# Both feed-forward layers by seven half-size products per 576-token batch, with weight operands streamed from DRAM

## The chip, the cores and the metric

One NeuronCore of a Trainium2 chip runs the whole program. The engines are named as in the profile: PE (TensorE), DVE (VectorE), ACT (ScalarE), POOL (GpSimd) and SP (SyncE, which here only issues DMAs). The metric is the device time of one execution in microseconds; lower is better. Everything is computed in fp32.

## The reference

Attention over 8 batches of 8 heads, 576 tokens, head size 64, with a threshold on the scores, then a feed-forward block over all 8 x 576 = 4608 tokens. The two feed-forward weights arrive as 64-bit floats.

```python
scores = q @ k.T / 8                                   # per batch and head, 576 x 576
scores = where(scores >= max(scores) - tau, scores, -1e9)
attn = exp(scores - max(scores)); attn /= sum(attn) + 1e-9
x = (attn @ v) as (4608, 512)                          # heads side by side
h = x @ w_in                                           # (4608, 512) @ (512, 2048)
out = (h / (1 + exp(-1.702 * h))) @ w_out              # (4608, 2048) @ (2048, 512)
```

## The kernel before, in words

**Attention.** The work goes by *pairs* of heads: 32 pairs, four to a batch. Of a pair `n`, `load_qk` and `load_v` fetch the data, `prep` (L522) transposes q and k in 32 x 32 blocks, `scores` (L538) makes the transposed scores in nine steps `j`, each four matmuls of 288 columns on the four 64 x 64 quarters of PE's array, and `keep` (L555) copies each step out of PSUM on ACT. Scores lie in tiles of two steps (1152 columns), the ninth step alone. `in_groups` (L561) takes maxima over keys on DVE, `sub` (L666) subtracts the row's threshold, `mask` (L672) and `exps` (L676) on ACT finish it, `in_groups` again sums, `values` (L687) multiplies by v on PE, and `place_x` (L789) divides and writes the result, already transposed, into `xT`. For pairs 0 to 4 the sums are made on PE (`sums_by_pe`). From pair 7 on (`JOINT`) the values of pair n - 2 and the scores of pair n run on PE in turn as one uninterrupted stretch.

**Feed-forward.** Tokens go in 18 blocks of 256, which don't match the batches of 576 (`cuts`). Three forms are used:

- Blocks 0 and 1, plain: `mm1_0` (L844, 256 columns), `tanh` on ACT, `gelu_0` on DVE (x times sigmoid as 0.5 x (1 + tanh)), `mm2` (L826, 512 columns).
- Blocks 2 to 13 (`feed_forward`): layer one plain in `mm1` (L804), layer two by seven products of half size (Strassen's scheme in Winograd's form) in `product` (L995). Its operand sums of the activations are made on POOL (`s_sums` L961 to L963, `s_last` L974), those of `w_out` once (`t_minus`, `t_plus`). DVE adds the products together as it reads them from PSUM (`read`, L1017).
- Blocks 14 to 17 in two pairs (`two_blocks`): both layers by seven products, layer one in `product1` (L909, read by `read1`, L925), layer two in `product`. The sums of `w_in` for this are made in SBUF that attention has left.

In a seven-product scheme a matrix product is cut into 2 x 2 quarters, and 7 products of quarters replace 8, at the price of sums of operands and of results.

**Weights.** Both weight matrices stay in SBUF from the start. Each of 32 pieces is loaded twice by POOL (L473, L474, 512 KB each, the second shifted by three bytes) and turned from 64-bit to 32-bit by three steps on DVE and one on ACT (`cv_ex` L484, `cv_power` L492, `cv_frac` L498 and L502, `cv_end` L510). Six staging places are in use.

**PSUM.** Two pools: `psA`, three tiles of two banks (scores, values, some products), and `psM`, two tiles of one bank (feed-forward, early sums).

**What sets the order.** Every step is a task with an engine, an assumed cost, a rank, predecessors and places that it takes and gives back. `run_in_order` simulates these tasks and lets each free engine take the ready task of lowest rank; the instructions are emitted in that order, so each engine's queue is fixed when the kernel is built. Attention tasks have rank `n` plus an offset by function name (`EARLY` for pairs 0 to 3, `SECOND` for 4 to 7, `LATER`, and `CV` for the conversions; ranks below zero get none). Matmuls of the feed-forward have rank 1000 (`LAST`), so on PE attention goes first whenever it is ready. `LEAD` = 6 holds attention back: the scores of pair n wait for feed-forward task 16 (n - 6), so attention runs some six pairs ahead and ends well before the feed-forward does.

Of the kernel before, what the change touches and what calls it, by code (L numbers as in the profile page):

```python
# [19 lines left out]
P = 128  # L20
# [10 lines left out]
def kernel(  # L31
# [13 lines left out]

# [3 lines left out]
    NPAIR = H // 2  # L69
    KT = P // 2  # L70
    NK = S // KT
    NKT = NK // 2
    SH = S // 2
    QB = S // 32
    BLK = 256
    BANK = 512
    HT = BLK // 2
    HF = d_ff // P // 2
    HM = d_model // 2
    NBLK = B * S // BLK  # L80
    NDC = d_model // P
    NFC = d_ff // P
    SCALE = 1.0 / math.sqrt(D)

# [4 lines left out]
    work = ctx.enter_context(tc.tile_pool(name="work", bufs=2))  # L89
# [3 lines left out]
    psA = ctx.enter_context(tc.tile_pool(name="psA", bufs=3, space=bass.MemoryType.PSUM))  # L93
    psM = ctx.enter_context(tc.tile_pool(name="psM", bufs=2, space=bass.MemoryType.PSUM))

    w_in = const.tile([P, NDC, d_ff], FP32, name="w_in")
    w_out = const.tile([P, NFC, d_model], FP32, name="w_out")

    N_T, N_G, N_S = 3 * HF * HM, NFC * BLK, 2 * HF * HT
    arena = const.tile([P, N_T + N_G + N_S], FP32, name="arena")
    tw = [arena[:, ts(x, HF * HM)].rearrange("p (j m) -> p j m", m=HM) for x in range(3)]
    g = arena[:, ds(N_T, N_G)].rearrange("p (f j t) -> p f j t", f=2, t=BLK)
    sg = [
        arena[:, ds(N_T + N_G + x * HF * HT, HF * HT)].rearrange("p (j t) -> p j t", t=HT)
        for x in range(2)
    ]
# [8 lines left out]
    minus = const.tile([P, 2, KT], FP32, name="minus")  # L117
    own_row = const.tile([P, QB // 2], FP32, name="own_row")
    shift = const.tile([P, 1], FP32, name="shift")

    tasks = []
    NXT = 5
    limits = {"psA": 3, "psM": 2, "s_m": 8, "s_t": 2, "io": 2, "hs": 2, "osb": 2, "xT": NXT, "mb": 1,
              "raw0": 1, "raw1": 1, "qkT0": 1, "qkT1": 1, "v_m0": 1, "v_m1": 1, "w64_0": 1, "w64_1": 1, "row": 1, "row_s": 1, "rc": 1}
    for x in ("raw0", "raw1", "qkT0", "qkT1", "mb"):
        limits[x + "_apart"] = 1  # L130
    limits["s_m_apart"] = NKT

    EARLY = {
        "exps": -17.61,
        "in_groups": 12.77,
        "keep": 26.48,
        "load_qk": 6.42,
        "load_v": 0.46,  # L140
        "mask": 4.73,
        "one_group": -15.86,
        "one_row": -9.06,
        "over_halves": -11.42,
        "over_tiles": -0.06,
        "place_x": -9.61,
        "prep": -11.56,
        "row_in": 31.26,
        "row_out": -12.68,
        "scores_run": 26.41,  # L150
        "spread_max": 4.27,
        "spread_sums": 4.87,
        "sub": 8.56,
        "sums_by_pe": -5.69,
        "sums_in": 2.27,
        "sums_out": 16.51,
        "turn_rows": -16.86,
        "turn_sums": -5.4,
        "values": 24.67,
        "w_sum": 2.1,  # L160
        "x_sum": -20.63,
    }
    SECOND = {
        "exps": -12.92,
        "in_groups": 29.73,
        "keep": 6.19,
        "load_qk": 1.9,
        "load_v": 13.07,
        "mask": 1.29,
        "one_group": 2.55,  # L170
        "one_row": -2.79,
        "over_halves": -24.79,
        "over_tiles": 9.26,
        "place_x": -19.31,
        "prep": -22.42,
        "row_in": -9.56,
        "row_out": -26.33,
        "scores_run": 2.45,
        "spread_max": 6.39,
        "spread_sums": -1.67,  # L180
        "sub": 27.62,
        "sums_by_pe": 38.88,
        "sums_in": 16.9,
        "sums_out": 8.98,
        "turn_rows": 12.04,
        "turn_sums": -0.33,
        "values": 2.02,
        "w_sum": -3.88,
        "x_sum": -12.22,
    }  # L190
    LATER = {
        "exps": 1.49,
        "in_groups": 1.97,
        "keep": -9.78,
        "load_qk": -5.98,
        "load_v": -3.59,
        "mask": 21.95,
        "one_group": 4.78,
        "one_row": -20.84,
        "over_halves": 8.94,  # L200
        "over_tiles": -3.1,
        "place_x": 4.68,
        "prep": -7.1,
        "row_in": 2.23,
        "row_out": -2.52,
        "scores_run": -13.43,
        "spread_max": -3.68,
        "spread_sums": -27.9,
        "sub": 9.4,
        "sums_by_pe": 4.28,  # L210
        "sums_in": 8.55,
        "sums_out": -0.12,
        "turn_rows": -4.72,
        "turn_sums": 8.12,
        "values": 0.63,
        "w_sum": 21.55,
        "x_sum": 7.65,
    }
    CV = {
        "cv_end": -26.29,  # L220
        "cv_ex": 6.34,
        "cv_frac": -13.49,
        "cv_power": -9.91,
        "load_w": 3.03,
# [4 lines left out]
    QUARTERS = ("scores", "scores_run", "again", "values", "sums_by_pe")  # L229
    ENTER = {True: 0.2, False: 0.22}  # L230

    def task(engine, cost, rank, f, *a, after=(), take=(), give=(), lag=None):
        if lag is None:
            lag = LAG[engine]
        if 0 <= rank < LAST:
            biases = EARLY if a[0] < NPAIR else SECOND if a[0] < 2 * NPAIR else LATER
            rank += CV[f.__name__] if f.__name__ in CV else biases.get(f.__name__, 0.0)
        tasks.append((engine, cost, rank, f, a, [x for x in after if x is not None],
                      take, give, lag))
        return len(tasks) - 1  # L240
# [103 lines left out]
    rebias = const.tile([P, 1], FP32, name="rebias")  # L344
    JOINT = 7
    TWICE = ()
    BY_POOL = {}

    APART = (1, 3)
    spare = arena[:, 8 * P * 4 :]
    offset = {"raw0": 0, "raw1": S, "qkT0": 2 * S, "qkT1": 3 * S, "mb": 4 * S}
    offset.update({f"s_m{t}": (6 + 2 * t) * S for t in range(NKT)})

    room, end = {}, 0
    for tag, size, bufs in (
        ("s_m", 2 * S, 8), ("s_t", S, 2), ("raw0", S, 1), ("raw1", S, 1), ("qkT0", S, 1),  # L360
        ("qkT1", S, 1), ("mb", S, 1), ("rc", S, 1), ("v_m", NK * 2 * D, 2),
    ):
        room[tag] = [(end + x * size, size) for x in range(bufs)]
        end += bufs * size
    arena2 = const.tile([P, end], FP32, name="arena2")
    held = {}

    def seat(tag, x=0):
        o, size = room[tag][x]
        return arena2[:, o : o + size]  # L370

    def home(n, tag, key=None):
        if n in APART:
            o = offset[key or tag]
            return spare[:, o : o + (2 if tag == "s_m" else 1) * S]
        return seat(tag)

    def seat_scores(n, t):

        if t < NKT and n in APART:  # L380
            return home(n, "s_m", f"s_m{t}")
        if n >= JOINT:
            tag, o, size = held[n, t] = held.pop((n - 2, t))
            return arena2[:, o : o + size]
        tag = "s_m" if t < NKT else "s_t"
        o, size = room[tag].pop(0)
        held[n, t] = tag, o, size
        return arena2[:, o : o + size]

    def free_scores(n, tiles=range(NKT + 1)):  # L390
# [5 lines left out]
    def own(n, *pools):  # L396
        return tuple(x + "_apart" for x in pools) if n in APART else pools


# [28 lines left out]
    WC = 512  # L428
    wide = moe_w_in.dtype != FP32
    pieces = [(w_in, moe_w_in, c, j) for j in range(d_ff // WC) for c in range(NDC)]  # L430
    n_in = len(pieces)
    pieces += [(w_out, moe_w_out, c, j) for c in range(NFC) for j in range(d_model // WC)]
# [1059 lines left out]
```

## Time and profile before

| | |
|---|---|
| runs | 1311.93, 1314.18, 1315.43 us; median 1314.18 |
| profiled execution, span from first to last instruction | 1309.8 us |
| median of the runs less that span | 4.4 us |
| mean granted clock of PE | 0.989 |
| DMA | 103.78 MB in 194309 packets, 160284 of them under 512 B |
| first feed-forward matmul (L844) | 113.9 us |
| first matmul of a block with seven products (L804) | 273.6 us |
| last write into `xT` (L789) | 1081.0 us |
| end of the last matmul | 1306.2 us |

The profiled execution lists a span and no time of its own; the runs' times hold 4.4 us beside it, by their median. In a group's line the profile gives the source line, engine, operation, operands with shapes, the count, then busy us and mean ns of one instruction, then the engine's idle time before them and what ended it. An fp32 matmul has two records, so counts of matmuls are half the records. DMA-issuing instructions don't count as busy.

### The profile page before, as it was taken

To read this page: it belongs to the slowest core of one execution; us is meant where nothing else is said; L and a number is where in the kernel's file an instruction comes from. 1 tells how busy PE (TensorE), PEld (TensorE's weight loads), DVE (VectorE), ACT (ScalarE), POOL (GpSimd) and SP (SyncE) were. 2 spreads that over 40 slices of the span, in tenths; PEclk is the share of its full clock that TensorE was granted. 3 is DMA by queue.
4 is the path that set the end of the run, shared out by engine and by line. 5 is a ranking of instruction groups with operands and counts; after the bars stand their busy time and mean duration, and the time that the engine had idled before them with its cause. 6 is when DMAs were issued, how large, how long until landed. Compare 5 with 4: busy or idle time off the path is not lost. (4 is left out here: it accounts for less than half of the span.)

```text
span 1309.8 us, 22824 instructions
## 1 busy us (share of the span) xinstructions
PE 1260.5 (96%) x9128; PEld 972.6 (74%) x9128; DVE 1002.2 (77%) x1601; ACT 646.6 (49%) x830; POOL 246.1 (19%) x300
## 2 busy tenths in 40 slices
PE   5869999999999999999999999999999999999998
PEld 2436854477688777777778888777777778888887
DVE  7999998989998877778877877777888864652642
ACT  5975656766664544455554545454556540210210
POOL 1301210022030212112020302020212117120120
PEclk8989999999999999999999999999999999999999
DMA  6976967264322222221222222222122110000000
GB/s 118 339 186 214 282 209 132 67 125 83 82 57 71 55 64 64 56 57 44 63 47 61 55 71 55 72 56 70 42 52 54 38 44 9 9 1 33 1 1 32
DMA packets 194309, 103.78 MB, mean 79 GB/s; under 512 B 160284, under 2 KB 171292, under 8 KB 194204
## 3 DMA queue, kind: packets, MB, share of 16 engines
q1 hardware_dynamic: 180476, 64.30, 20.6%
q0 software_dynamic: 11360, 37.74, 9.7%
q8 instruction: 71, 1.16, 0.4%
q10 hardware_dynamic: 2368, 0.30, 0.2%
q14 instruction: 34, 0.28, 0.1%
HBM read 88.40 MB, written 9.70 MB: 75 GB/s over the span
## 5 line engine op out<-in xcount | busy, mean ns | idle before, releaser
L561 DVE TRANSPOSE_TENSOR_REDUCE part<-arena 128x36 f32<-128x1152 f32 x295 | 361.5, 1241 | 45.9 <-ACT arena L555 32.3
L804 PE MATMUL hps<-xT,w_in 128*128 128x256 f32 x1536 | 336.9, 380 | 0.4 <-DVE arena L816 0.4
L804 PEld LDWEIGHTS hps<-xT,w_in 128*128 128x128 f32 x1536 | 290.8, 190 | 45.5 <-issue 5.7
L672 ACT ACTIVATE arena<-arena 128x1152 f32<-128x1152 f32 (+1 forms) x160 | 169.4, 1058 | 144.9 <-DVE arena L666 144.6
L555 ACT COPY arena<-ps 128x576 f32<-128x576 f32 x288 | 170.4, 647 | 121.2 <-PE ps L538 120.9
L666 DVE TENSOR_TENSOR arena<-arena 128x1152 f32<-128x1152 f32 (+1 forms) x158 | 197.5, 1281 | 19.6 <-DMA arena<-row 19.5
L995 PE MATMUL ops<-w_out,arena 128*128 128x256 f32 x896 | 202.9, 381 | 1.2 <-DVE arena L816 1.1
L676 ACT ACTIVATE arena<-arena,shift,scl 128x1152 f32<-128x1152 f32 (+1 forms) x160 | 200.1, 1251 | 4.1
L538 PE MATMUL ps<-arena 64*64 64x288 f32 x2304 | 174.1, 419 | 25.1 <-DVE arena L522 14.4
L995 PEld LDWEIGHTS ops<-w_out,arena 128*128 128x128 f32 x896 | 169.0, 190 | 29.1 <-DVE arena L816 3.7
L961 POOL TENSOR_TENSOR arena<-arena 128x256 f32<-128x256 f32 x56 | 50.8, 907 | 658.4 <-DVE arena L816 556.7
L687 PE MATMUL pv<-arena 64*64 64x288 f32 x2176 | 161.2, 410 | 0.0
L538 PEld LDWEIGHTS ps<-arena 64*64 64x64 f32 x2304 | 83.7, 137 | 93.6 <-ACT arena L555 30.7
L995 PE MATMUL ops<-arena 128*128 128x256 f32 x672 | 150.6, 380 | 0.0
L813 ACT ACTIVATE th<-hps 128x512 f32<-128x512 f32 x112 | 66.0, 589 | 167.9 <-PE hps L804 148.2
L995 PEld LDWEIGHTS ops<-arena 128*128 128x128 f32 x672 | 127.3, 190 | 19.3 <-issue 2.2
L687 PEld LDWEIGHTS pv<-arena 64*64 64x64 f32 x2176 | 82.0, 135 | 55.3 <-issue 12.8
L1017 DVE SCALAR_TENSOR_TENSOR osb<-ops,osb 128x256 f32<-128x256 f32 x98 | 39.5, 414 | 91.8 <-PE ops L995 85.0
L816 DVE SCALAR_TENSOR_TENSOR arena<-th,hps 128x512 f32<-128x512 f32 x96 | 64.1, 667 | 37.1 <-ACT th L813 37.0
L844 PE MATMUL hps<-xT,w_in 128*128 128x256 f32 x256 | 57.3, 382 | 1.3 <-DVE arena L850 1.2
L826 PE MATMUL ops<-w_out,arena 128*128 128x512 f32 x128 | 56.4, 596 | 0.0
L844 PEld LDWEIGHTS hps<-xT,w_in 128*128 128x128 f32 x256 | 48.1, 190 | 11.0 <-DVE arena L850 3.0
(117 smaller groups left out, 1027.8 us busy)
## 6 DMA issues: line engine op xcount, KB each, us to landing
arena<-in_v_dram SPq DMA_DIRECT2D x128, 144.0 KB
arena<-in_q_dram SPq DMA_DIRECT2D x128, 72.0 KB
out_dram<-osb SPq DMA_DIRECT2D x36, 256.0 KB
arena<-in_k_dram SPq DMA_DIRECT2D x124, 72.0 KB
arena<-row SPq DMA_DIRECT2D x62, 144.0 KB
arena<-row_s SPq DMA_DIRECT2D x54, 144.0 KB
w_out<-in_moe_w_in_dram POOLq DMA_DIRECT2D x12, 512.0 KB, 9.4
arena<-in_moe_w_out_dram POOLq DMA_DIRECT2D x12, 512.0 KB, 5.9
```

The source lines that it names most:

```text
L538: nc.tensor.matmul(ps[ts(c, KT), h, 0:SH], lhsT=mats[n, 1][ts(h, D), ts(j, KT)], rhs=mats[n, 0][ts(h, D), ts(c, SH)], start=True, stop=True,)
L555: nc.scalar.copy(out=sT[n, t][:, u], in_=pss.pop((n, j))[:, :, 0:SH])
L561: nc.vector.tensor_reduce(out=stats[n, op][:, t * 2 * QB : min(2 * t + 2, NK) * QB], in_=sT[n, t].rearrange("p u h (g d) -> p (u h g) d", ...
L666: engine.tensor_tensor(out=s, in0=s, in1=mbs[n].unsqueeze(1).to_broadcast(list(s.shape)), op=ALU.subtract)
L672: nc.scalar.activation(out=s, in_=s, func=AF.Prelu, alpha=STEEP)
L676: nc.scalar.activation(out=s, in_=s, func=AF.Exp, scale=scl, bias=shift)
L687: nc.tensor.matmul(o[c][ts(h, D), 0:SH], lhsT=left(j, h)[ts(c, KT)], rhs=sT[n, t][ts(c, KT), u, h, :], start=(j == 0), stop=(j == NK - 1),)
L804: nc.tensor.matmul(hidden[j][:, ts(f, BLK)], lhsT=w_in[:, c, ds((f * HF + j) * P, P)], rhs=xTs[blk][:, c, :], start=(c == 0), stop=(c == N ...
L813: nc.scalar.activation(out=ths[j], in_=hidden[j], func=AF.Tanh, scale=GELU_SCALE / 2)
L816: nc.vector.scalar_tensor_tensor(out=g[:, :, j, :], in0=two(ths.pop(j)), scalar=1.0, in1=two(hidden.pop(j)), op0=ALU.add, op1=ALU.mult,)
L844: nc.tensor.matmul(hidden[j][:, ts(i, BLK)], lhsT=w_in[:, c, ts(j, P)], rhs=xTs[i][:, c, :], start=(c == 0), stop=(c == NDC - 1),)
L995: nc.tensor.matmul(banks[blk][k][:, ts(o, HM)], lhsT=left[:, j, :], rhs=right[:, j, :], start=(j == 0), stop=(j == HF - 1),)
```

## The change

- Feed-forward goes by batches of 576 tokens instead of blocks of 256. All matmuls of it have 288 columns (half a batch).
- The first batch is plain (`product0`, `product00`, 16 x 8 matmuls each). The other seven go by seven products in both layers: `product1` for four pairs of row blocks `jp`, `product2` for two column halves `i`. Results come out transposed, are turned on DVE (`turn_out`) and stored in runs of 32 numbers.
- Weights: the 32 pieces are quarters, four to a *quad*; eight quads. They are converted into `weights`, the first batch uses them there; POOL makes the four sums of each quad (`w_sum`), and the seven operands of each quad go to DRAM (`store_base`, `store_sums`). Every later batch loads them again in *cells* of two 512-column operands, seven cells in a ring (`load_cell`, issued by POOL). The SBUF of `weights` then holds `g`.
- Sums of x (`x_sum`) and of g (`g_sum`, four per `jp`), and the gelu of two of four quarters, go on POOL; for the latter ACT adds the one (`plus_one`). DVE does the other two and all reads from PSUM.
- One PSUM pool of four slots with two banks serves everything. `values` of a pair, scores and products all take a slot.
- Attention's tiles are three of three steps (1728 columns) instead of four of two and one of one; `place_x` is one instruction.
- Loads of weights use three staging places instead of six. Pairs 4 and 5 load q and k into free space of `xT`.
- All offsets of ranks are replaced, and `LEAD` becomes 5.38, counted in feed-forward time (27.16 us per pair); the sums of `w_out` in SBUF, the `two_blocks` form and unused variants go.

The core of the diff:

```diff
-    psA = ctx.enter_context(tc.tile_pool(name="psA", bufs=3, space=bass.MemoryType.PSUM))
-    psM = ctx.enter_context(tc.tile_pool(name="psM", bufs=2, space=bass.MemoryType.PSUM))
+    psum = ctx.enter_context(tc.tile_pool(name="psum", bufs=1, space=bass.MemoryType.PSUM))
+    TILES = (3, 3, 3)
+    NCELL = 7
+    NHS = 5
+    slots = [0, 2, 4, 6]
...
+    def load_cell(key):
+        _, kind, x, k = key
+        c = at[key] = cells.pop(0)
+        if kind == 0:
+            rows = w_dram[x].rearrange("p (a w) -> p a w", w=U)
+            rows = (rows[:, 0:4:3], rows[:, 1:5:3], rows[:, 5:7], rows[:, 2:3])[k]
+            o = cell(c).rearrange("p (a w) -> p a w", w=U)
+            CELL_ON.dma_start(out=o[:, 0 : rows.shape[1]], in_=rows)
...
+    P1, P6, P2, P7, P5, P3, P4 = range(NQ)
+    def product1(b, jp, x):
+        b11, b12, b21, b22 = (x_quarter(b, d, t) for d in range(2) for t in range(2))
+        right = {P1: b11, P6: xsum[1], P2: b21, P7: b12, P5: xsum[0], P3: b22, P4: xsum[2]}[x]
+        c = cell(at[b, 0, jp, x // 2])[:, ts(x % 2, U)].rearrange("p (c j f) -> p c j f", c=2, j=2)
+        bank = banks[x] = slot()
+        for u in range(2):
+            for d in range(2):
+                nc.tensor.matmul(
+                    ps_all[:, bank + u, 0:SH], lhsT=c[:, d, u, :], rhs=right[:, d, :],
+                    start=(d == 0), stop=(d == 1),
+                )
...
+    SUMS = {P6: (1, 0), P2: (0, 0), P7: (2, 1), P3: (1, 1), P4: (2, 2)}
+    def read1(x, part=0):
+        ps = scored(banks[x])[:, :, 0:SH]
+        if x == P1:
+            hs[0] = hs_free.pop(0)
+            nc.scalar.copy(out=hs[0], in_=ps)
...
+        o, i = SUMS[x] if x != P5 else ((1, 1), (3, 2))[part]
+        nc.vector.tensor_tensor(out=hs[o], in0=ps, in1=hs[i], op=ALU.add)
...
+    G_SUMS = ((4, 1, 0), (5, 3, 4), (1, 3, 1), (6, 2, 5))
+    def g_sum(jp, k, engine):
+        o, a, c = (g[:, jp, y] for y in G_SUMS[k])
+        engine.tensor_tensor(out=o, in0=a, in1=c, op=ALU.subtract)
...
+    def product2(b, i, x, h):
+        right = {P1: 0, P6: 5, P2: 2, P7: 1, P5: 4, P3: 3, P4: 6}[x]
+        c = cell(at[b, 1, i, x])[:, ts(h, U)].rearrange("p (j m) -> p j m", m=P)
+        for j in range(4):
+            nc.tensor.matmul(
+                ps_all[:, banks[x], 0:SH], lhsT=c[:, j, :], rhs=g[:, 2 * h + j // 2, right, j % 2, :],
+                start=(j == 0 and h == 0), stop=(j == 3 and h == 1),
+            )
...
+    def store(b, i, m, o):
+        for y in range(4):
+            nc.sync.dma_start(
+                out=out[ds(b * S, S), ds((2 * m + i) * P + 32 * y, 32)].rearrange(
+                    "(t a) m -> a t m", a=32
+                ),
+                in_=ot[o][ts(y, 32)].rearrange("p (t m) -> p t m", m=32),
+            )
...
-    LEAD = 6
+    LEAD = 5.38
+    W_RANK = (-11.09, -0.32, 24.62, -9.57, -4.22, 9.2, 81.56, -23.12)
+    CELL_ON = nc.gpsimd
+    X_ON, G_ON, T_ON, W_ON = "POOL", ("POOL", "DVE", "POOL", "DVE"), "POOL", "POOL"
...
+        for jp in range(NJP):
+            loads = [load((b, 0, jp, y), [jp], 2.0 if y < 3 else 1.0) for y in range(4)]
...
+            for y in range(4):
+                after = [gs[jp, z] for z in range(4)] + ([tsum[jp, y - 1]] if y else [])
+                tsum[jp, y] = task(
+                    T_ON, 1.45 if T_ON == "POOL" else 0.67, FIRST, g_sum, jp, y, engines[T_ON], after=after,
+                )
...
+                for h in range(2):
+                    after = ffn[-1:] + [a]
+                    for jp in (2 * h, 2 * h + 1):
+                        if x in (P1, P2, P3):
+                            after.append(gs[jp, {P1: 0, P2: 2, P3: 3}[x]])
+                        else:
+                            after.append(tsum[jp, {P6: 1, P5: 0, P7: 2, P4: 3}[x]])
...
+    PER_PAIR = 32 * NQ * FF / NPAIR
```

## The prediction

> **What bounds the kernel now.** I read four views in this order: the busy times of the whole execution, the chain that ended last, the waits of TensorE, and the busy times cut into stages. The cuts are the first feed-forward matmul (113.9 us), the first one of a seven-product block (273.6), the last attention write into `xT` (1081.0) and the end of the last matmul (1306.2).
>
> ```profile
> PE 1260.5 (96%) x9128; PEld 972.6 (74%) x9128; DVE 1002.2 (77%) x1601; ACT 646.6 (49%) x830; POOL 246.1 (19%) x300
> ```
>
> TensorE (PE) is busy 96% of 1309.8 us. Busy matmuls overlap in the records, so I check this against spacing. In the chain that ended last the columns are start, length, line, count:
>
> ```profile
> 1257.80 24.17 PE ops L995 x112
> 1281.98 24.19 PE ps L995 x112
> ```
>
> A matmul has two records, so 56 matmuls of 256 columns take 24.17 us: 0.4316 us each. In the middle, attention runs values and scores in turn:
>
> ```profile
> 604.06 1.15 PE L538 MATMUL ps<-arena 64*64 64x288 f32 x16
> 605.03 1.15 PE L687 MATMUL pv<-arena 64*64 64x288 f32 x16
> 606.00 1.15 PE L538 MATMUL ps<-arena 64*64 64x288 f32 x16
> ```
>
> Sixteen records are two sets of four quarter-array matmuls, and the next set starts 0.97 later: a pass of 288 columns takes 0.485, which is also 0.4316 x 288/256. So both column counts have a price.
>
> ```profile
> 0.00:113.90 113.90, 76.22 (x1008) 40.71 (x1008) 102.16 (x178) 85.34 (x108) 20.89 (x52) 0.90 0.78 215
> 113.90:273.60 159.70, 155.66 (x1037) 96.45 (x1034) 145.81 (x237) 93.56 (x119) 21.04 (x34) 0.99 0.63 173
> 273.60:1081.00 807.40, 803.57 (x6049) 638.14 (x6048) 650.35 (x989) 439.33 (x547) 149.52 (x162) 1.00 0.26 60
> 1081.00:1306.20 225.20, 225.09 (x1042) 197.31 (x1040) 103.49 (x202) 28.35 (x56) 54.63 (x52) 1.00 0.03 11
> ```
>
> After length come PE, weight load, VectorE (DVE), ScalarE (ACT), GpSimd (POOL), clock, DMA share, GB/s. PE idles 37.7 us before the first feed-forward matmul, where DVE is 90% busy, and only 8 us in all behind it. From 273.6 on I can rebuild the time: 1888 feed-forward matmuls (in units of 256 columns) x 0.4316 = 815, 22 pairs of scores and 24 of values x 9 x 0.485 = 201, sum 1016 of 1032.6; the rest is mode changes and 4 us of idle. **PE is the bound from 114 us to the end**; attention's other engines fit beside it.
>
> **The change, part by part.** The sum goes against the profiled 1309.8, which lies 4.4 below the median of 1314.18; I add that back.
>
> *Matmuls.* Before: 2 plain blocks 256 (128 in `mm1_0`, 64 of double width in `mm2`), 12 blocks x (64 `mm1` + 56 `product`) = 1440, 2 double blocks x (112 `product1` + 112 `product`) = 448; 2144 x 0.4316 = 925.3 us. After: first batch 16 x 8 + 16 x 8 = 256 of 288 columns, seven batches x (4 x 7 x 4 + 2 x 7 x 8) = 224 each, 1824 x 0.485 = 884.6. Attention keeps its passes (32 x 18, sums of 5 pairs). **-40.7 us**, all on the path. Weight loads (190 ns each) stayed under the spacing of 216 ns and have 242.
>
> *Start.* Before 113.9 DVE converts 16 pieces of `moe_w_in` at 0.42 + 0.43 + 0.70 + 0.69 = 2.24 us, 36 us in all. After, the loads go in one chain through three staging buffers, and quad 2 stands at rank 24.6 behind early attention; only quad 0's four pieces (with quads 0 and 1, eight) must be done by the first product. Seven or eight conversions moved behind that point free up to 16 us of DVE, but the next stage has DVE at 91% and must take them. Against it: 14.7 MB of operands are written to DRAM, and pieces are read in rows of 1 and 2 KB instead of 4. The first two stages used 0.78 x 113.9 + 0.63 x 159.7 = 189 us of all 16 DMA engines out of 273.6; 14.7 MB at the rate of queue 0 below is 49 more, the accumulating copies that go give back 13. 225 still fits. Bounds -12 and +15; I take -3, nearer to no change, since what moves lands in a nearly full stage.
>
> *VectorE and PSUM.* By the forms of the groups:
>
> ```profile
> L925 DVE TENSOR_TENSOR arena<-ps,arena 128x256 f32<-128x256 f32 x68 | 27.5, 421 | 15.9 <-PE ps L909 15.0
> L961 POOL TENSOR_TENSOR arena<-arena 128x256 f32<-128x256 f32 x56 | 50.8, 907 | 658.4 <-DVE arena L816 556.7
> L974 POOL TENSOR_TENSOR arena<-arena 128x512 f32<-128x512 f32 x28 | 35.6, 1271 | 102.3 <-PE ops L995 102.3
> ```
>
> Pieces of `place_x` (L789) grow 1.06 ns per column, so a read of 576 columns is 0.76 us. Per batch: 28 such reads 21.3, 8 gelus x 0.75 = 6.0, 14 reads of 288 x 0.45 = 6.3, 4 transposes x 0.745 = 3.0: 36.6, against 2.25 x (8 x 0.676 + 7 x 0.424) = 18.9 before. Tiles of three give back 5 (an L561 of 1728 columns is 1.97; 24 fewer starts). So +13 us per batch, and DVE goes from 81% to some 91% while attention runs. Between 360 and 393 us the present kernel has DVE at 97% with PE at 100% (31.7 and 32.7 of 32.7 us), so this can be hidden; I charge **+3**, bounds 0 and +15. All four PSUM slots of two banks now serve both users, and a product needs 1.94 us where its read needs 0.76 (P5: 1.5), so reads keep up on average.
>
> *GpSimd and the handover.* 28 operations of 576 columns (727 ns at 256 and 1271 at 512 in undisturbed calls give 1.41) are 39 us a batch, and 30 issues of cells at 0.54 to 0.65 are 18: 40% of some 145 us, but 80% of layer one's 54 when no attention stretches it. Layer two's P6, second half, needs g sums of the last pair of rows: after the last P4, read 0.76, tanh 0.69, plus one 0.69, gelu 1.41, two sums 2.82, and 0.1 to 0.15 for each handover between engines (an L925 ended at 1123.58, its L929 began at 1123.68), 0.6 in all: 7.0 us. PE has three half products, 5.8. Stall **1.2 per batch**. While pairs remain, an attention block (18 x 0.485 and two mode changes, 9.2 us) can stand there; I charge the last two batches: **+2.5**, bounds 0 and +8 (seven batches).
>
> The Trainium skill (SBUF — State Buffer, Who interferes with whom) speaks against moving these sums to GpSimd: a VectorE instruction with two SBUF inputs and a GpSimd instruction that reads SBUF exclude each other, and the later one waits. The trace agrees: L961 takes 717 ns at least and 1783 at most, L666 up to 1892 where its median is 1351. By that rule, 20 such VectorE calls a batch meeting GpSimd 27% of the time for 0.7 us would add an estimated 4 us of VectorE work a batch; without it nothing. The sum above stands without either.
>
> *Weight stream.*
>
> ```profile
> q1 hardware_dynamic: 180476, 64.30, 20.6%
> q0 software_dynamic: 11360, 37.74, 9.7%
> ```
>
> Queue 0 moved 37.74 MB in 9.7% of 1309.8, 297 GB/s; a batch streams 30 cells, 14.7 MB, 49 us or 34%. Output leaves in 9216 pieces of 128 B a batch; queue 1's packets, nearly all small, took 24 ns each on one engine: 14 us, 9%. With the present 26% that is 69% of the engines. Transfers of 512 KB landed in 3.7 to 12.7 us (medians by group); seven cells of 3.9 us of PE work are 27 us of lead. **0**; hidden by that lead, and if it went, each cell late by 0.2 us would cost 42.
>
> *End.* Behind the last matmul now 3.65 us (a read of 0.42 and a store). After: read 0.45, transpose 0.745, four stores of small packets: about 6. **+2.5**.
>
> Sum: -40.7 - 3 + 3 + 2.5 + 2.5 = -35.7; 1309.8 + 4.4 - 35.7 = **1278.5**.
>
> **Rivals.** *The start gains more.* PE idles 37.7 us there and DVE's conversions are what fill it; if eight move at full price and stage two still hides them, -13 in place of -3, and no wait on DVE later: 1265.5. For it: the first batch now brings 124 us of matmuls in place of 110, so the second batch's pairs have 14 us longer (their last `xT` write came at 268, 5 us before it was needed). Against: stage two's DVE 91%. *VectorE and GpSimd eat half.* All seven handovers stall (+8) and queues behind 1.97 us reductions hold PSUM slots (+15): 1296. For it: the 80% and 91% above; against: the slices at 97%. *Slower: cells come late.* One mechanism: `load_cell` stands in GpSimd's own order behind sums that wait for VectorE and ScalarE, and its transfer shares the engines with small packets. While a cell is late PE stands still. It decides from a mean of 0.17 us per cell (35.7/210) on; at 0.4, 84 us against that gain: 1362.5. For it: nothing in this trace streams during the matmuls, and DMA was 0.99 busy between 33 and 65 us. Against: 69% and 27 us of lead.
>
> **How the numbers follow.** Likeliest 0.56 (own range 1268 to 1299: from -40.7 and +2.5 with the start from -8 to +8, DVE and handover together 0 to 15); better start 0.11; half eaten 0.16, of which 0.05 ends within 0.3% (what a measurement of this kernel can tell from no change, 4 us); late cells 0.17. Faster 0.56 + 0.11 + 0.11 = 0.78, same 0.05, slower 0.17. The range 1258 to 1312 holds the first three and leaves out the fourth and a little at the ends.
>
> **What would show it.** Right: feed-forward matmuls 0.485 apart, PE idle under 15 us between the first product and the end, first product between 100 and 120 us, DVE near 90% in the middle. Wrong: PE waiting on a transfer from `w_dram` (late cells); PE or its weight loads waiting on g sums of GpSimd once a batch for more than 2 us; VectorE at 97% with PE idle beside it; a first product after 130 us.

## The result and the profile after

The changed kernel takes 1357.6 us (median of 4, 1353.9 to 1360.9); the kernel before 1313.1 (4 runs, 1311.7 to 1315.4). The ratio is 1.034 (95%: 1.032 to 1.036). The prediction was 1278.5, 79 us too low and on the wrong side. The profiled execution has a span of 1356.4 us and a mean granted clock of 0.964 (0.989 before).

The busy times of the whole execution:

```profile
PE 1246.6 (92%) x8616; PEld 886.3 (65%) x8616; DVE 1069.1 (79%) x1335; ACT 650.0 (48%) x744; POOL 566.6 (42%) x512
```

PE has 512 records fewer than before and its busy time is 14 us less, but idle time grew. VectorE has 266 instructions fewer and works 67 us longer.

The same execution in stages, cut at the first feed-forward product, the first product of seven, the last matmul of attention and the last matmul. After length come PE, weight load, VectorE, ScalarE, GpSimd, clock, DMA share, GB/s:

```profile
0.00:122.70 122.70, 78.22 (x1008) 43.75 (x1008) 110.61 (x147) 79.79 (x89) 38.03 (x46) 0.85 0.74 208
122.70:312.50 189.80, 175.04 (x1164) 123.32 (x1161) 164.75 (x207) 94.96 (x107) 71.82 (x70) 0.96 0.82 227
312.50:1193.00 880.50, 835.79 (x5802) 596.48 (x5801) 746.35 (x907) 455.37 (x518) 390.72 (x332) 0.98 0.58 145
1193.00:1350.70 157.70, 157.50 (x648) 122.78 (x648) 46.20 (x75) 19.84 (x31) 66.02 (x67) 1.00 0.46 128
```

The last row is the best evidence on the feed-forward alone: 0.2 us of idle in 157.7, at full clock, while cells stream at 128 GB/s. The loss lies where attention runs: 14.8 us of PE idle in the second stage, 44.7 in the third (before: 4.0 and 3.8 in the stages that correspond), and the clock falls to 0.96 and 0.98 there. What PE waited for in the third stage (total, times, longest):

```profile
PE ps L559 <- DVE hx L786: 32.8, 14, 8.3
PE ps L766 <- DVE hx L786: 3.5, 2, 2.4
```

Scores (L559) wait for a PSUM slot that holds a finished feed-forward product, because VectorE has not read it yet (L786). Why VectorE has not, its own waits in that stage say:

```profile
DVE seats L646 <- DMA seats<-row: 49.3, 17, 6.2
DVE hx L907 <- PE ps L884: 25.6, 14, 3.3
DVE hx L786 <- PE ps L766: 17.1, 16, 3.7
```

L646 is `sub`, attention's subtraction of the threshold. The thresholds of a pair are written to DRAM in two times 18 short rows (`row_out`, L632) and read back spread over the partitions (`row_in`, L641); the subtraction waits for that. Over the whole run VectorE waits 57.6 us for rows, at most 6.6 at a time; before, it waited 19.5 us, at most 2.7 at a time. One stall in the timeline, first VectorE, then PE, then SyncE's queue (start, length, line):

```profile
321.62 0.43 DVE L587 TENSOR_REDUCE red<-part 128x18 f32<-128x162 f32 x1
...
323.48 0.73 DVE L876 STREAM_TRANSPOSE ot<-th 128x576 f32<-128x576 f32 x1
324.81 3.83 DVE L646 TENSOR_TENSOR seats<-seats 128x1728 f32<-128x1728 f32 x2 [0.59 <-DMA seats<-row]
328.55 0.75 DVE L786 TENSOR_TENSOR hx<-ps,hx 128x576 f32<-128x576 f32 x1
```

```profile
319.88 1.20 PE L559 MATMUL ps<-seats 64*64 64x288 f32 x16 [1.68 <-DVE seats L542]
329.35 1.24 PE L559 MATMUL ps<-seats 64*64 64x288 f32 x8 [8.28 <-DVE hx L786]
```

```profile
318.32 0.65 SPq L632 DMA_DIRECT2D row<-flat  x2
320.75 1.10 SPq L641 DMA_DIRECT2D seats<-row  x2
```

The row went out at 318.32 and the subtraction started at 324.81. Two subtractions then stand ahead of one 0.75 us read in VectorE's queue, and PE stands still for 8.28 us until that read is done. The wait itself shows as only 0.59 us of idle on VectorE; its cost is where it sits in the queue.

The subtraction is also longer than before, and GpSimd's sums are longer than the 1.41 us I had counted:

```profile
L646 DVE TENSOR_TENSOR seats<-seats 128x1728 f32<-128x1728 f32 x90 | 196.8, 2202 | 57.6 <-DMA seats<-row 57.6
L820 POOL TENSOR_TENSOR mem<-mem 128x576 f32<-128x576 f32 x112 | 192.7, 1741 | 3.7 <-DVE mem L805 1.5
```

The median subtraction takes 1957 ns and the longest 3173: some are held up, others not at all.

In the second stage most of PE's 14.8 us of idle are waits for VectorE's activations of the first batch (L843), 9.7 us in all; the two largest groups:

```profile
PE ps L559 <- DVE mem L843: 4.7, 2, 2.8
PE ps L666 <- DVE mem L843: 3.7, 1, 3.7
```

The single wait of 3.7 us (until 172.5) is the pattern above: L843 stands behind a subtraction that had waited 6.6 us for a row. The longer two of the others (1.8 us until 190.7, 2.8 until 223.2) have no row in them: L843 stands behind conversions and attention's instructions without a gap. In this slice VectorE is busy for 97% of the time and PE for 76%:

```profile
169.50:203.40 33.90, 25.60 (x170) 15.98 (x171) 32.86 (x45) 18.32 (x20) 12.81 (x13) 0.80 0.80 251
```

### The profile page after: what moved, and what is told of

Same layout as the page of the kernel before. It is cut to its first block, busy times and chain, and to the rows that moved or that the text cites. A ratio compares the mean times of both kernels' runs of the same rounds, so it can differ in the third digit from the quotient of the medians.

```text
span 1356.4 us, 22147 instructions
## 1 busy us (share of the span) xinstructions
PE 1246.6 (92%) x8616; PEld 886.3 (65%) x8616; DVE 1069.1 (79%) x1335; ACT 650.0 (48%) x744; POOL 566.6 (42%) x512
## 4 chain that ended last, share of the span: by engine, by line
DVE 39%; PE 24%; DMA 12%; issue 10%; ACT 7%; SPq 3%; POOL 3%; DVEq 0%; POOLq 0%; ACTq 0%
DVE part L579 13%; PE ps L766 9%; PE ps L884 8%; DMA seats<-row 7%; DVE seats L646 6%; PE ps L666 4%; DVE hx L786 4%; PE ps L559 4%; DMA row<-flat 2%; ACT seats L656 2%; POOL mem L820 2%; ACT seats L652 2%; DVE flat L607 2%; SPq L407 2%; DVE fold L601 2%
## 5 line engine op out<-in xcount | busy, mean ns | idle before, releaser
L884 PE MATMUL ps<-mem 128*128 128x288 f32 x1568 | 387.1, 409 | 1.2 <-ACT seats L573 1.0
L884 PEld LDWEIGHTS ps<-mem 128*128 128x128 f32 x1568 | 298.5, 191 | 88.8 <-ACT seats L573 5.8
L579 DVE TRANSPOSE_TENSOR_REDUCE part<-seats 128x54 f32<-128x1728 f32 x171 | 331.2, 1954 | 23.1 <-ACT seats L573 16.8
L646 DVE TENSOR_TENSOR seats<-seats 128x1728 f32<-128x1728 f32 x90 | 196.8, 2202 | 57.6 <-DMA seats<-row 57.6
L766 PE MATMUL ps<-xT,mem 128*128 128x288 f32 x896 | 234.5, 409 | 3.5 <-DVE hx L786 3.5
L559 PE MATMUL ps<-seats 64*64 64x288 f32 x2160 | 163.8, 429 | 64.8 <-DVE hx L786 32.8
L766 PEld LDWEIGHTS ps<-xT,mem 128*128 128x128 f32 x896 | 169.7, 191 | 55.5 <-ACT seats L573 5.3
L820 POOL TENSOR_TENSOR mem<-mem 128x576 f32<-128x576 f32 x112 | 192.7, 1741 | 3.7 <-DVE mem L805 1.5
L573 ACT COPY seats<-ps 128x576 f32<-128x576 f32 x270 | 155.7, 649 | 80.1 <-PE ps L559 79.1
L786 DVE TENSOR_TENSOR hx<-ps,hx 128x576 f32<-128x576 f32 x196 | 142.7, 744 | 58.7 <-PE ps L766 44.5
L766 PE MATMUL ps<-hx,mem 128*128 128x288 f32 x672 | 177.3, 407 | 0.0
L559 PEld LDWEIGHTS ps<-seats 64*64 64x64 f32 x2160 | 80.8, 140 | 134.9 <-DVE hx L786 40.7
L666 PE MATMUL ps<-seats 64*64 64x288 f32 x2160 | 156.6, 424 | 1.1 <-ACT seats L656 1.1
L666 PEld LDWEIGHTS ps<-seats 64*64 64x64 f32 x2160 | 83.4, 139 | 59.8 <-issue 11.0
```

The costliest lines, as they stand in the source:

```text
L559: nc.tensor.matmul(ps_all[ts(c, KT), x + h, 0:SH], lhsT=mats[n, 1][ts(h, D), ts(j, KT)], rhs=mats[n, 0][ts(h, D), ts(c, SH)], start=True, ...
L573: nc.scalar.copy(out=sT[n, t][:, j - FROM[t]], in_=scored(x)[:, :, 0:SH])
L579: nc.vector.tensor_reduce(out=stats[n, op][:, FROM[t] * QB : FROM[t + 1] * QB], in_=sT[n, t].rearrange("p u h (g d) -> p (u h g) d", d=32) ...
L646: nc.vector.tensor_tensor(out=s, in0=s, in1=mbs[n].unsqueeze(1).to_broadcast(list(s.shape)), op=ALU.subtract)
L666: nc.tensor.matmul(o[c][ts(h, D), 0:SH], lhsT=left(j, h)[ts(c, KT)], rhs=sT[n, t][ts(c, KT), u, h, :], start=(j == 0), stop=(j == NK - 1),)
L766: nc.tensor.matmul(ps_all[:, bank + u, 0:SH], lhsT=c[:, d, u, :], rhs=right[:, d, :], start=(d == 0), stop=(d == 1),)
```

## The experiments

Three theories. **One**: the stream of cells shares the DMA engines with the rows' trip through DRAM, the rows land late, and VectorE's subtraction blocks its queue. **Two**: VectorE's and GpSimd's element-wise work exclude each other. **Three**: VectorE's load and the planned order alone. Each kernel below ran once, beside a run of the kernel before (1312.4 to 1316.8); the four runs of the changed kernel lie 7 us apart, so small differences in time are not read. The kernels of the table leave out data or work and give wrong results, to take one cause away; none of them changes an assumed cost, a rank or a predecessor, so the planned order is the changed kernel's in all of them.

| kernel | us | wait for rows at `sub`, us | mean `sub`, ns | VectorE busy, us |
|---|---|---|---|---|
| changed kernel | 1357.6 | 57.6 | 2202 | 1069.1 |
| few bytes in the cells | 1328.3 | 18.5 | 2212 | 1068.8 |
| rows not awaited from pair 8 on | 1327.6 | 6.3 | 2211 | 1065.7 |
| small GpSimd work | 1332.5 | 48.6 | 2050 | 1033.3 |
| the same with two fills | 1326.7 | 45.4 | 2048 | 1034.7 |
| small weight sums, but the first block's | 1344.7 | 54.3 | 2160 | 1051.7 |
| small weight sums, all | 1350.0 | 56.5 | 2138 | 1050.2 |
| few bytes, small GpSimd work | 1309.0 | 14.2 | 2055 | 1034.4 |
| these and all weight sums small | 1298.2 | 11.0 | 1988 | 1016.9 |

### Few bytes in the cells

```diff
-            CELL_ON.dma_start(out=o[:, 0 : rows.shape[1]], in_=rows)
+            F = U if len(full) < NCELL else 32
+            full.append(key)
+            CELL_ON.dma_start(out=o[:, 0 : rows.shape[1], 0:F], in_=rows[:, :, 0:F])
```

and the same for the cells of layer two.

> Every weight cell after the first seven brings only 32 of each 512 columns (the rest of the cell is left as it was, so the feed-forward results are those of stale weights); the same DMAs, in the same program order, with 1/16 of the bytes. Theory 1 (the cell stream lies in the DMA engines beside the threshold rows' trip through DRAM, VectorE's subtraction waits for the row at the head of its queue, and the reads of the products behind it keep PSUM full): the wait for the row at L646 between 312 and 1201 us falls from 49.3 to about 15 us, and the time to 1305-1325. Theory 2 (GpSimd's and VectorE's element-wise work get in each other's way) and theory 3 (the order of VectorE's queue and its load alone): 1350-1360, and the wait for the row stays at 40 or more.

Measured 1328.3, and the wait for rows fell to a third. The line of the group in this kernel:

```profile
L651 DVE TENSOR_TENSOR seats<-seats 128x1728 f32<-128x1728 f32 x90 | 197.7, 2212 | 18.5 <-DMA seats<-row 18.5
```

The instruction itself did not get shorter, only its wait. Theory one explains 29 us, less than I expected of it, and not all of the loss.

### Long rows in the stores

```diff
-        for y in range(4):
-            nc.sync.dma_start(
-                out=out[ds(b * S, S), ds((2 * m + i) * P + 32 * y, 32)].rearrange(
...
+        nc.sync.dma_start(
+            out=flat_out[ds((2 * m + i) * P * S, P * S)].rearrange("(p x) -> p x", x=S),
+            in_=ot[o],
+        )
```

> Each output tile is stored by one DMA of 128 rows of 2304 bytes (into the right batch, but not in the output's layout) in place of four DMAs in pieces of 128 bytes. Theory 1 in its form by the stores (their issue on SyncE's queue, 2.3 to 5.4 us a tile, and their small packets hold up the rows): 10 to 25 us less, 1333-1348, and the wait for the row at L646 at 35 or less. Theory 1 by the cells, theories 2 and 3: within 5 us of 1357.

1357.1, and the wait for rows 57.9. The 128-byte stores cost nothing that this run shows.

### No trip through DRAM

```diff
-    BY_DMA = (0, 1, *range(3, NP))
+    BY_DMA = ()
```

> All thresholds are spread by VectorE's transpose instead of by the trip through DRAM (both kernels do that for one pair of 32 only). It costs VectorE some 0.8 us a pair by the planner's own costs, 25 us in all, and takes the wait for the row (57.6 us) away. Theory 1: the gain exceeds the cost, 1325-1348. Theory 3 (VectorE's load is the bound): the cost shows in full, 1370-1390. Theory 2: between, 1355-1370.

1350.7: the wait is gone, but the order differs, and the result lies between the ranges of the theories. From the first product of seven to the end it takes 1016 us (1044 in the changed kernel); before that point it loses 20. Undecided by itself.

### Small GpSimd work

```diff
-        o, a, c = (g[:, jp, y] for y in G_SUMS[k])
+        F = SH if seen_b[0] < 2 else 16
+        o, a, c = (g[:, jp, y, :, 0:F] for y in G_SUMS[k])
```

and the same in `x_sum` and in GpSimd's `gelu`.

> From the third batch on GpSimd's subtractions of x, its activations and its sums of them work on 16 of each 288 columns (the rest of those operands is stale), so GpSimd's own time falls from 1.4-1.8 us an instruction to some 0.2. Theory 2: VectorE's subtraction at L646 falls from 2.20 to 1.96 us and the time by 25 to 45 us, to 1313-1333. Theory 1: VectorE's instructions get the same 0.24 us shorter but the wait for the row stays at 40 us or more, and the time falls by less than 10 us, 1348-1357. Theory 3: 5 to 15 us less, by the shorter subtractions.

1332.5, the subtraction at 2050 ns, VectorE's busy time 36 us less, while the wait for rows stays at 48.6. So theory two has its own 25 us.

### Both

> Both edits together: 32 of 512 columns in each weight cell after the first seven, and GpSimd's element-wise work from the third batch on at 16 of 288 columns (the feed-forward results are those of stale operands). Alone they gave 29.3 and 25.1 us. Theory A (two separate losses, the late threshold rows and GpSimd's work beside VectorE's, which add up): 1300-1308, the wait for the row at 15-20 us, VectorE's subtraction at 2.05 us. Theory B (both edits relieve the same stall, VectorE at the head of its queue): 1318-1328.

1309.0, 1 us above the first range: 48.6 of the 54.4 that would be the sum. The two losses are nearly separate.

### Small weight sums

```diff
-        engine.tensor_tensor(out=o, in0=a, in1=c, op=op)
+        F = U if x == 0 else 32
+        engine.tensor_tensor(out=o[:, 0:F], in0=a[:, 0:F], in1=c[:, 0:F], op=op)
```

> GpSimd's sums of weight quarters (L507) work on 32 of 512 columns after the first block, so their 1.7 us become some 0.2 (the second factors of four products are stale). If the start is late because these sums and VectorE's subtraction disturb each other there (four of them took 11.8 us at 56 us, beside three subtractions that took 7.8): the first batch's first product at 112-118 us, where it was at 122.7, and 5-10 us less, 1347-1353. If the start is bound by the 32 conversions on VectorE and the landing of their halves: 121-124 us, and within 3 us of 1357.

1344.7, but the first product still at 121.3. The edit kept the first block's sums whole, and just these lie in the start, so the question of the start was not answered; the gain came in the second stage (189.8 to 180.8 us). Hence the next kernel, with `F` = 32 for all blocks:

> As the kernel with small sums of weight quarters, but for all eight blocks, the first too, whose sums fell into the first 60 us (its four sums and three subtractions beside them took 11.8 and 7.8 us); the buffer is set to zero at the start, and the operands that these sums make are stale. If the late first product (122.7 against 113.9 us before) is due to these sums beside VectorE: first product at 112-118, time 1334-1341. If it is due to what VectorE has to do there (conversions, five pairs' reductions and subtractions): 119-122, time 1341-1347.

First product at 119.5, in the second reading's range: what VectorE has to do there sets the start, and the sums only lengthen it. The time, 1350.0, is in neither range and 5 us above that with the first block whole, which shows how much a single run scatters. The start's subtractions before the first product, in the changed kernel and in this one:

```profile
L646 DVE TENSOR_TENSOR mem<-mem 128x1728 f32<-128x1728 f32 x6 | 13.5, 2308 | 0.0
L646 DVE TENSOR_TENSOR seats<-seats 128x1728 f32<-128x1728 f32 x6 | 13.5, 2302 | 0.0
```

```profile
L646 DVE TENSOR_TENSOR mem<-mem 128x1728 f32<-128x1728 f32 x6 | 11.5, 1970 | 2.1 <-DMA mem<-row 2.1
L646 DVE TENSOR_TENSOR seats<-seats 128x1728 f32<-128x1728 f32 x6 | 11.4, 1961 | 0.0
```

Four microseconds of VectorE's time, and the start is 3.2 us shorter. The weight sums cost 8 to 13 us in all, a third of it in the start.

### Three causes together

> The three edits together: weight cells of 32 of 512 columns after the first seven, GpSimd's element-wise work at 16 of 288 columns from the third batch on, and all its sums of weight quarters at 32 of 512 columns (the feed-forward results are those of stale operands). If the three causes make up the miss of the prediction and add up: 1285-1297, near the 1278.5 that was predicted for the change. If 15 us or more of the miss have another cause (the order of the joint attention stretch and the start): 1298-1309.

1298.2, just outside the first range: 59.4 of the 79 us. Its second and third stages take 177.2 and 837.5 us, its first product comes at 118.8.

### Which way the bytes act

With rows by DRAM for pairs 0 to 7 only, first with whole cells, then with few bytes:

```diff
-    BY_DMA = (0, 1, *range(3, NP))
+    BY_DMA = (0, 1, *range(3, 2 * NPAIR))
```

> The trip through DRAM stays for pairs 0 to 7 but 2, as in the changed kernel; the 24 pairs from 8 on have their thresholds spread by VectorE. With all 32 so, the part from the first product of seven to the end was 28 us shorter and the part before it 20 us longer. Theory 1 (rows late beside the cells): that gain without that loss, 1322-1338. If the gain came with the other order in the first 330 us (what was done there was not left for later): 1345-1357.

1345.5: 12 us gained, less than theory one asked for and just inside the range of the other reading. The order differs here, and VectorE is busy 47 us longer (1116.0 against 1069.1). Whether the rows are the whole way in which the bytes act can't be read from it, but from the next kernel, which has few bytes as well:

> The trip through DRAM for pairs 0 to 7 only (alone 1345.5) and 32 of 512 columns in each weight cell after the first seven (alone 1328.3; feed-forward results of stale weights). If the cells' bytes cost time only by making the rows late: from pair 8 on there is no row left to be late, and the few bytes give nothing, 1340-1347. If the stream costs time in another way too: 10 us less or more, 1316-1336.

1348.9 against 1345.5: where no row from pair 8 on can be late, the bytes cost nothing that shows. Then the wait alone, in the changed kernel's own order and with all its transfers:

```diff
+            in1=(mbs[n] if n < 2 * NPAIR else ones[:, 0:1].to_broadcast([P, S]))
+            .unsqueeze(1).to_broadcast(list(s.shape)),
```

> In the changed kernel's own order, with its rows still sent through DRAM and its cells whole, the subtraction of pairs 8 to 31 reads a constant in place of the row (wrong thresholds), so it waits for no transfer. If the stream costs time through the late rows alone, this gives back what the few bytes gave (29) or, since rows that came in time with few bytes still cost 10 us of waiting, some more: 1318-1332. If the waits at L646 are harmless (something else is late at the same time) and the bytes cost in another way: 1345-1358.

1327.6, where few bytes gave 1328.3. Its group line:

```profile
L646 DVE TENSOR_TENSOR seats<-seats,ones 128x1728 f32<-128x1728 f32 x72 | 158.1, 2211 | 0.0
```

Same instruction, same mean, no wait. Taken together, few bytes, rows not awaited and the two kernels with rows early show the path: 103 MB of cells cost some 30 us, through rows that come late, and nothing beyond that stands out of the scatter. Last, the same kind of load on the kernel before:

```diff
+        for t in dummy:
+            c = turns[0] % 4
+            turns[0] += 1
+            nc.gpsimd.dma_start(
+                out=t.bitcast(U32).rearrange("p (a w) -> p a w", w=512),
```

> The kernel before, with three transfers of 512 KB from DRAM to DRAM on GpSimd's queue behind each of its sums of activations (168 in all, 84 MB, in rows of 2 KB; nothing reads them). If a stream of that size delays what attention brings and sends through DRAM: the waits for rows grow from 19.5 to 30 us or more and the time by 8 to 30 us, 1321-1343. If the kernel before has room for it and the rows matter only with the changed kernel's fuller VectorE and joint PSUM slots: less than 5 us more, 1312-1318.

1358.2 against 1316.8 beside it, 41 us, above both ranges. The subtraction in the kernel before, then with the stream:

```profile
L666 DVE TENSOR_TENSOR arena<-arena 128x1152 f32<-128x1152 f32 (+1 forms) x158 | 197.5, 1281 | 19.6 <-DMA arena<-row 19.5
```

```profile
L668 DVE TENSOR_TENSOR arena<-arena 128x1152 f32<-128x1152 f32 (+1 forms) x158 | 197.2, 1279 | 58.4 <-DMA arena<-row 58.2
```

The wait grows by 38.7 us and the time by 41. The kernel before had room on VectorE (77% busy) and separate PSUM pools, and was hit as hard. These transfers also write DRAM and stand in GpSimd's queue, so the 41 is not the price of the cells; that rows come late beside such a stream is shown in both kernels.

### Which way GpSimd acts

```diff
+        if F < SH:
+            fill(engine, g[:, jp, G_SUMS[k][0], :, F:])
...
+    def fill(engine, o):
+        for _ in range(4):
+            engine.memset(o, 0.0)
```

> As the kernel with GpSimd's feed-forward work at 16 of 288 columns (1332.5), but each activation and sum is followed by four fills of the other 272 columns with zero, which keep GpSimd busy and read nothing (the feed-forward results are those of zeroed operands). If GpSimd costs time by excluding VectorE while it reads SBUF: VectorE's subtraction at L646 stays near 2.05 us and the time at 1328-1338. If it costs time by being busy, its results and the buffers it frees coming late, or if fills exclude VectorE as well: 1345-1365, with the subtraction at 2.15 or more in the last case.

1406.7, far above both ranges, the subtraction at 2058 ns. Four fills (552 ns each) and a short sum (460) make some 2.7 us, longer than the 1.74 they replace, and PE now waits for GpSimd itself:

```profile
PE ps L900 <- POOL mem L765: 20.4, 5, 5.3
```

So this run showed that a late GpSimd is costly, not whether it had been late. With two fills:

> As with four fills, but two: with the 0.62 us of the short sum they make 1.7 us, the 1.74 of the changed kernel's sums (four made 2.8, so that GpSimd was later than in the changed kernel). With GpSimd as busy as in the changed kernel but reading nothing long: if exclusion from SBUF is what costs the 25 us, 1328-1340 with the subtraction at L646 near 2.06; if GpSimd's being busy is, 1350-1362 with the same 2.06.

1326.7, although GpSimd is busy for 506.9 us (340.0 without fills, 566.6 in the changed kernel) and a short sum with its two fills takes some 1.5 us:

```profile
L646 DVE TENSOR_TENSOR seats<-seats 128x1728 f32<-128x1728 f32 x90 | 182.9, 2048 | 45.6 <-DMA seats<-row 45.4
L765 POOL MEMSET mem<- 128x544 f32 x288 | 158.5, 550 | 8.3
```

A GpSimd that is nearly as busy but mostly only writes costs nothing that shows. So the 25 us go with its full-length sums and activations, which read SBUF beside VectorE's work. Of the 36 us by which VectorE's busy time falls with small GpSimd work, 13.7 are the subtraction's (196.8 to 183.1); 11.8 belong to two small instructions of 18 columns, of which L601 goes from 389 to 268 ns and L705, a copy with one input, from 230 to 196.

### Other orders

> The same work and the same trip through DRAM, but the order is planned with durations from the changed kernel's profile: the row lands 3 us later (the mean wait of the subtractions that waited), subtraction 2.2, GpSimd's sums 1.74, its activations 1.6, VectorE's activations 0.82, its reads 0.74 and 0.45, weight sums 1.72 us. Theory 3 (the loss is head-of-queue waiting from an order planned with too short costs): the waits at L646 fall below 25 us and the time to 1325-1345. Theory 1 and 2 in their hard form (VectorE and the DMA engines have no room left, whatever the order): 1350-1362.

1378.9, slower by 21 and above both ranges, with the first product at 132.6. The wait for rows falls to 38.3 us, but PE's largest wait is now 27.1 us for ScalarE's copies of scores (L573). Truer costs in the planner gave a worse order here.

```diff
-    LEAD = 5.38
+    LEAD = 4.44
```

> LEAD 4.44 in place of 5.38, nothing else: each pair's scores may start 0.94 x 27.2 = 25.5 us of feed-forward work later, so attention's VectorE work spreads over a longer stretch and into the last one, where VectorE is 30% busy. If VectorE's load in the middle (84% with its waits on rows) is what makes its waits cost time: 8 to 20 us less, 1338-1350. If only the length of the row's trip and the exclusion by GpSimd count, each as often as before: 1354-1361.

1379.4, again above both ranges. Row waits are unchanged (50.3 in the third stage), and PE waits 29.2 us for copies of scores. With rows early:

> LEAD 4.44 and the trip through DRAM for pairs 0 to 7 only (with that alone 1345.5). By VectorE's load: the two gains add up, as the spread thresholds cost VectorE 0.8 us a pair, which the longer stretch has room for: 1325-1338. If not: 1342-1350.

1351.3, 6 us more than with rows early alone. And attention earlier (`LEAD` = 6.2, rows early):

> LEAD 6.2 in place of 5.38, with the trip through DRAM for pairs 0 to 7 only (alone 1345.5): attention may run 22 us earlier. Moved 25.5 us later it cost 5.8 us (and 21.8 with all rows by DRAM). If that cost is a slope: 1335-1343. If it was the scatter of another planned order, whichever way it is moved: 1346-1365.

1381.9, above both ranges; here PE waits 23.1 us for GpSimd's sums (L820), the handover that the prediction feared and that the changed kernel doesn't have. Moved either way, the order got worse, so these four runs speak for scatter among planned orders, of 6 to 36 us, not for a rule on VectorE's load. By that scatter the gains of no trip (7 us) and rows early (12) can't be read closely either. Theory three isn't refuted by them; in the third stage it has only shown no lever, while in the second stage PE did wait for a VectorE without a gap. No version that computes everything came near the kernel before; the best was 1345.5.

## Why the prediction was wrong, step by step

- **Matmuls, -40.7: right where it can be seen alone.** The feed-forward stretch without attention has 0.2 us of idle at full clock, and four product matmuls follow one another by 1.94 us, 0.485 each. In the other stages, where PE pauses, the granted clock is lower (0.96 and 0.98) and the matmuls' records are longer.
- **Weight stream, 0: the step that failed first.** I asked only whether a cell could come late for PE, and 27 us of lead answered that rightly: PE waited for no cell. I did not ask what the stream makes late. The rows' trip was in front of me: 19.5 us of waits in the kernel before, and queue 1's small packets in my own sum of DMA shares. An average of 69% of the engines was taken as room. The runs put this term at 29 to 30 us (few bytes, rows not awaited).
- **VectorE and PSUM, +3: mis-sized.** The reads take what was worked out (744 ns for 576 columns, 447 for 288). But the loss from exclusion was left out of the sum. The Trainium skill (SBUF — State Buffer, Who interferes with whom) was weighed for an estimated 4 us of VectorE work a batch; the runs show 36 us of it in the six batches with small GpSimd work, 6 a batch, so the estimate worked out from that rule was low, and leaving it out of the sum was worse. The same section says that a GpSimd instruction that only writes does not disturb a two-input VectorE instruction: the kernel with two fills agrees (2048 ns, against 2050 without fills and 2202 with sums). On the path it is 25 to 31 us. The cited slice of 97% DVE beside 100% PE showed that one stretch of the kernel before could hide such a load; the changed kernel's slice at 97% has PE at 76%.
- **Start, -3: wrong sign.** The first product came at 122.7, not 110.9, within the bounds I gave (-12 to +15). The gain was to come from seven or eight conversions moved behind it, eight of 16 being left in front. Both counts were off. The last step of a conversion (L510 before, L493 after) ran 13 times ahead of the first product before and 11 times after:

```profile
L510 DVE SCALAR_TENSOR_TENSOR w_in<-w_out 128x512 f32<-128x512 int32 x9 | 6.2, 687 | 0.0
L510 DVE SCALAR_TENSOR_TENSOR w_in<-arena 128x512 f32<-128x512 int32 x4 | 2.7, 688 | 0.2 <-ACT arena L492 0.2
```

```profile
L493 DVE SCALAR_TENSOR_TENSOR mem<-hx 128x512 f32<-128x512 int32 x8 | 5.4, 681 | 1.1 <-ACT hx L476 1.0
L493 DVE SCALAR_TENSOR_TENSOR mem<-mem 128x512 f32<-128x512 int32 x3 | 2.0, 678 | 0.0
```

  VectorE is busy for 110.6 us of the start, where it was 102.2 before, which is nearly all of the 8.8 us by which the first product is later. 3.2 us of the lateness are the weight sums beside VectorE; how the rest divides between conversions and attention's work there stays open.
- **Second stage, no term of its own: mis-sized.** It held 14.8 us of PE idle where 4.0 were in the kernel before, most of it waiting for VectorE's activations (9.7 us). I had called the stage nearly full, with VectorE at 91%, but drew from it only a smaller gain for the start and no cost for PE. The weight sums explain 6 to 9 us of its length; my sum had them nowhere.
- **Handover, +2.5: too high.** PE waited 0.2 us for GpSimd's sums in the last stage and not at all in the third.
- **End, +2.5: right.** 5.7 us behind the last matmul.
- **Rivals.** Late cells did not happen. "VectorE and GpSimd eat half" named the right engines but another way, stalled handovers and reads queued behind long reductions, and lay 17.5 us above the likeliest time; by the runs GpSimd's work beside VectorE's cost 33 to 44. No rival had the stream delaying others.
- **The signs.** PE idle between first product and end was to be under 15 us; it was 59.7. Of the four alarms one rang, and only in the second stage: VectorE at 97% with PE idle beside it. The others did not: no wait on cells, none on sums above 0.6 us, first product before 130. In the third stage, where most was lost, no alarm fitted: VectorE was busy 85% of the time, and with 6% of waiting on rows that was enough, because the waiting stood at the head of its queue.

The miss of 79 us: about 30 rows late beside the stream, 25 to 31 exclusion by GpSimd's feed-forward work, 8 to 13 exclusion by the weight sums, together 59 as measured in one kernel. Some 20 are left. In that kernel the first product comes 8 us later than predicted (118.8 against 110.9), and PE still idles 7.8 us in the second stage (4.0 in the kernel before) and 15.9 in the third (3.8). That this idle time comes from an order planned for other costs is a guess; no run settled it.

## What to carry to other kernels

When a change adds a large transfer stream, ask not only whether the stream comes in time but which small transfers on the same engines have a reader at the head of an in-order queue: list every wait on a transfer in the profile of before, and let each grow by some microseconds. When work moves to GpSimd, count its instructions that read SBUF as lost time for VectorE's instructions beside them, also in stages where GpSimd itself is never waited for. And a pause of 0.6 us in a queue can cost 8 on PE, so read who stands behind the waiting instruction rather than how long it waits.

## What the runs showed of the hardware

- The rows' trip through DRAM (2.2 KB out for each half of a pair, a spread copy back) took 6.5 us from the first issue to its use beside the stream (318.32 to 324.81). The longest wait for a row was 2.7 us in the kernel before and 7.7 in it with the transfers from DRAM to DRAM; in the changed kernel it was 6.6 in the second stage and 6.2 in the third, beside the cells. The Trainium skill (DMA: Bandwidth & Descriptors, Queues, rings and completion order) says that each engine takes its queues in turn, a whole packet of descriptors at a time; a short row behind packets of the cells' longer rows fits that, but no run here splits the delay.
- One subtraction of 1728 columns took 1908 to 3173 ns (mean 2202 beside GpSimd's full sums, 2050 with small ones), and one sum of weight quarters 1264 to 3006. Both sides lose.
- A GpSimd fill of 544 columns took 550 ns. Beside the fills the subtraction's mean stayed at 2048 to 2058 ns, but the small copy L705 took 196 ns without them, 210 with two and 276 with four.
- The granted clock went with PE's pauses: 0.98 in the third stage of the changed kernel, 0.99 with few bytes, and PE's busy time there fell from 835.8 to 822.8 us for the same matmuls. Of the 27 us by which that stage got shorter, half was idle time and half shorter matmuls.
